# Attention and two MLPs on one Trainium2 core: another form of the first MLP's denominator, and a new written-out order

## The chip, the core and the metric

The kernel runs on one core of one Trainium2 chip. The metric is the device time of one launch in microseconds, as the median of the runs. A kernel's trace gives the time and place of every instruction of its engines: PE (TensorE matmuls), PEld (PE's weight loads), DVE (VectorE), ACT (ScalarE), POOL (GpSimd) and SP (SyncE, which issues the DMAs here).

## The reference

Three steps follow each other, on 1536 rows of 512 numbers (two batches of 768):

```python
# 1. attention, 8 heads of 64: 16 neighbours to each side, and one summary for each block of 32 keys
k_sum = k.reshape(B, H, nb, block, D).max(axis=3)
v_sum = v.reshape(B, H, nb, block, D).mean(axis=3)
...
x = softmax(concat(local scores, summary scores + log 32)) @ concat(v, v_sum)
# 2. the first MLP
h = x @ w_in                                   # 512 -> 2048
P = a[0] + a[1] * h + a[2] * h2 + a[3] * h3    # h2 = h*h, h3 = h2*h
Q = 1.0 + np.abs(b[0]) * np.abs(h) + np.abs(b[1]) * h2
x = (P / (Q + 1e-06)) @ w_out                  # 2048 -> 512
# 3. the second MLP, with the same weight shapes
h = x @ w_in
y = (h * np.clip(h + 3.0, 0.0, 6.0) / 6.0) @ w_out
```

## The kernel before

**Accuracy and pieces.** Every large matmul is done as three: a number is split into a high part (the program's type F32R) and a low rest, and high x low, low x high and high x high are summed in PSUM. One product of the first layer (`first_product`, L637) is 12 matmuls of 128x512 for 128 hidden features and 512 tokens; its four output pieces (`second_product`, L654) are 3 matmuls each. In the second MLP 7 products of a Strassen scheme replace 8 (`product`, L812), the third token chunk is done plainly (L939), and output pieces have line L850. Weights arrive as 64-bit numbers and are rebuilt by `convert` (a clamp on POOL or DVE, a Prelu on ACT, a shift L311 and an or L313 on DVE) and `split` (a cast L286 or L322 and a subtraction L325).

**Attention** works in 12 groups of 128 tokens, six of each batch. `scores(g)` (L507) puts 64 small matmuls into two PSUM banks; `top` (L520, DVE) adds the mask and takes the maximum; `softmax` does exp on ACT (L534), sums (also L538 on DVE), a guard 1e-9 (L546), a reciprocal (L552) and the division (L549); `turn` (L574) transposes the two halves on PE, with a copy out (L577, L578); `values` (L591) multiplies by v, and x is written as high and low part (L601, L603). Token chunk 0 is groups 0 to 3, chunk 1 groups 4 to 7 and chunk 2 groups 8 to 11. `bank()` gives the PSUM banks: the scores of groups 0 to 3 use the four y banks, the others hs2 and hs3, which values and the v averages use too.

**The averages of v** of the first batch (`v_sums0`, L432 and L434) are summed over all six v tiles in bank hs3, with a matrix of 1/32 that is loaded by DMA in two forms (`blkw_sb` and `blk_sb`; `consts2`). Four copies (L445) and one or two more (L452, L453) or small DMAs (L449) put them into the v tiles as rows 96 to 119. `v_sums1` (L471) does the second batch.

**The first MLP's activation** (`act1`) is run 16 times on one product of 128x512 (the first 16 products, n < SINGLE), then 16 times on a pair of 128x1024. It takes q = |h| from PSUM (L701, ACT), u = |b1| q + |b0| (L704 on POOL or DVE, L707 on ACT), q = q u (L717, POOL or DVE), t = a3 h + a2 (L721, ACT), two DVE steps with h from PSUM (L723, L724), 1/(1+q) by Ln and Exp on ACT (L728, L730) with a Newton step (L735, L737), the high part (L739, ACT) and the low part (`low`, L745).

**The order** is written out by hand. The program first lists all steps (`Plan.add`: an engine, planned microseconds, a function, what it reads and writes); some steps have several engines to choose from. `PICK` holds the choice for each of these, one digit each, and `ORDER` the order in which all steps are issued, two characters each. Every engine, SP's DMA queue among them, works through its own part of that order and waits where something that it needs is missing. The planned microseconds serve for that plan and for `idle`, which puts matmuls of zeros on PE (L1045, into a free bank) where the plan leaves PE idle for over 0.6 us.

**The tail.** `evac2` (L865) adds the last output pieces into `part` and stores each 128x512 piece (256 KB) on SP (L869).

Of the kernel before, what the change touches and what calls it, by code (L numbers as in the profile page):

```python
# [59 lines left out]
ORDER = (  # L60
    "###(#4#)#;#$#2#6#0#8#%%>#9#:#5#&%E#3#<#'#7#W#1%Z#V$&%?#?#B$(%@$7$'$.%A%F$8#=$)#@$9#A%L%H$Y%G$*$/%B$0"
    "$?%I#+$+$,&%$-$:$H$@$1$A&#$2%J$3$;&$$B%K$<$5$4$C&7$=%C$I#F#C$6$>%S$J$K#D&&#>$F#E$D&'$P%M#G$E%D$Z%N%#"
    "#H%$&0&)%O$L$Q&8$R%P#*#,$M&U&9#I&:%T'#%)$N%%&;#-%&%V$O&<#J$S%*%Q%'#K&=%+%U$T#.'H$G%($U#L#N$W$V#X#O%,"
    "#Z%W%.%-#P$#%2$X#Y#Q&3&Y&*#R%0&V&W%5&1%3&,#S%/%4%8%1'$%R%6%;%9%7%X#/'I':%<%:%Y(Y&+%=#T&2&-&>'J'K&4$%"
    "&.*X'L&5&/&?'M$$&@&D&(&Z&A&I'N&E&X+.+$&F(,&J&G&K&B'%&H*Y';&L&C')#M&M+%&N&6&P+/&O&Q+&*Z+2'<&R+0'.+#'*"
    "+<&S+3(-+''/(/+1(.&T#U+('B+4'&'++=+)'0+5',+*'-+J+@'1''+6'2'((H++'5+A+>'3+7'6+?+,'=+B(M(I+-,$+C'V'>+8"
    "'D+K(%+D+9'O'4+E+L'7+F+N+M(N+:+X+O'8(O,#+G(J+Q+;+Y'W,%'A+R+Z(P'Y,&'?'X,4'@'9'C+H(&,5(Z'Z,('P)#,2+I('"
    ")8'E(#(K+P(L(Q,3'G($'Q,E'F),(T(:,G(():(0(R(U+S,D(S'R,F)'+T(V'S+U(1,6()+V)()-,'(*).+W))(W'T(;)*)/,),X"
    "(2,:(X,Y(<(=)0)$,+,*)+(>'U,H)%,,)&,7(+(3)>,;,-,8(A)1)3(?,V)2)4(@,L,W,<)C)5)?,.,/,Z,9)6,I)@)D(6)E,0)7"
    ",J,=,M,K)A,>);,N)F,?,1,O-4)<)Q-#)O-&,@1Z)B)G)9)=(B-',P-1,A(C-2-(-5-$)J-8)P(D-3(4-%1L-0(5,Q)H,B-F-9)I"  # L70
    ',C)K-:-),R)Z(E(7-B-*,S)L-J-+-E,T*#-,-G-C,U)M(8-X-K)U-6)N--*$*%-7-D(9-Y)R.$)V-L)W1S-H-..%1M-;-U)X1O-I'
    "(F)S-W-<-T2%1N(G)T.6-M*&)Y2)-=*.-N*0-/*9-V->-O*'.1-?*(*).7-P...:-Q.0***:.&*/*;*4./-Z1P*+.8.;-R.H.#*<"
    ".<-@*,-A.'*-*5.22*1V*1.31T.(.4*6.L.Z*=*21U*3*G-S.).I*@*7.F/#.**8.5.X.+/&.E.9*L/'.D.M*>.J.W2#.=.V.K.>"
    '*H*M.N.G.,*?*A.Y*I.?2$/4*N.O.@.-.P.A*O.Q*B/5.R/$.S/3*E.B/%/(*F/1*C*J2&/8/2/6.T/F/9*K*P*D.C/)2,/*/7*S'
    "/0/+*T.U2+*Q/C1W*R/G/E/,/;*U/-/J/H/D/</I*V/W1Q*W/V1X/:1R/B/./K/X/M/=2I2'///N2-/>2./Y/L/O/?/P/@/U0&/Q"
    "0#2(0*052L2W0'/R0+0(0,/S0%060)2J/A0-2/0./T2X3&2K0/0$1Y0G0900080C2P/Z2Y010D0:070H020F0=0<0I0E0;030>0?"
    "2Z0J0R3)2M0K3#2N0L0@0S2O3$040A3'0M3%0U1$0N0T3X1(1%0X3J0Y0O1)1&143(1*3Y2Q0Q1'132R0B1+0P4#0V1,3*0Z1=1-"
# [1039 lines left out]
```

## Time and profile before

| | us |
|---|---|
| median of the 3 runs | 589.68 |
| the lowest and the highest | 589.3, 591.37 |
| the profiled execution | 589.21 |
| its span, from the first to the last instruction | 587.4 |
| PE busy / weight loads | 578.6 / 466.6 |
| DVE busy | 494.4 |
| ACT busy | 348.5 |
| POOL busy | 294.7 |

The profiled execution is 1.8 us longer than its span, and 0.5 us below the median. Matmuls are pipelined, so that PE's busy time says little about its pace; pace is read from how many matmuls end in a stretch. Idle time of an engine that does not hold the others up costs nothing.

### The profile page before, as it was taken

To read this page: it belongs to the slowest core of one execution; us is meant where nothing else is said; L and a number is where in the kernel's file an instruction comes from. 1 tells how busy PE (TensorE), PEld (TensorE's weight loads), DVE (VectorE), ACT (ScalarE), POOL (GpSimd) and SP (SyncE) were. 2 spreads that over 40 slices of the span, in tenths; PEclk is the share of its full clock that TensorE was granted. 3 is DMA by queue.
4 is the path that set the end of the run, shared out by engine and by line. 5 is a ranking of instruction groups with operands and counts; after the bars stand their busy time and mean duration, and the time that the engine had idled before them with its cause. 6 is when DMAs were issued, how large, how long until landed. Compare 5 with 4: busy or idle time off the path is not lost.

```text
span 587.4 us, 9645 instructions
## 1 busy us (share of the span) xinstructions
PE 578.6 (98%) x3608; PEld 466.6 (79%) x3613; DVE 494.4 (84%) x887; ACT 348.5 (59%) x648; POOL 294.7 (50%) x272
## 2 busy tenths in 40 slices
PE   8999999999999999999999999999999999999997
PEld 4477788888888888888888888888888888888886
DVE  5999999999989898988899998968687786866643
ACT  3988998988676677658657455524540434424410
POOL 1777676573475657654766472131423175523210
PEclk9999999999999999999999999999999999999999
DMA  8986534301222223110000141320313023002005
GB/s 311 352 306 209 192 118 151 104 30 35 73 71 73 76 101 110 37 36 2 17 20 1 37 143 37 107 73 0 144 32 113 1 73 126 18 0 73 1 1 214
DMA packets 17983, 53.10 MB, mean 90 GB/s; under 512 B 2273, under 2 KB 2785, under 8 KB 17937
## 3 DMA queue, kind: packets, MB, share of 16 engines
q1 hardware_dynamic: 17936, 52.49, 26.1%
q8 instruction: 28, 0.46, 0.3%
q14 instruction: 19, 0.15, 0.1%
HBM read 48.55 MB, written 3.15 MB: 88 GB/s over the span
## 4 chain that ended last, share of the span: by engine, by line
PE 94%; DMA 2%; DVE 1%; SPq 1%; issue 1%; POOL 0%; ACT 0%; DVEq 0%
PE y L654 23%; PE y L850 22%; PE hb L637 15%; PE hc L812 13%; PE hs L637 8%; PE hc L939 7%; PE hs L591 2%; PE hs L507 2%; PE hs L574 1%; DMA mask_sb<-in_masks 1%; DMA k<-in_blk 1%; SPq L280 1%; DVE s L520 0%; POOL s L549 0%; PE hs L434 0%
## 5 line engine op out<-in xcount | busy, mean ns | idle before, releaser
L654 PE MATMUL y<-g,wt 128*128 128x512 f32 x576 | 139.1, 392 | 0.0
L654 PEld LDWEIGHTS y<-g,wt 128*128 128x128 f32 x576 | 106.8, 188 | 22.3 <-POOL g L745 0.3
L850 PE MATMUL y<-wt,g 128*128 128x512 f32 x480 | 116.1, 389 | 0.0
L850 PEld LDWEIGHTS y<-wt,g 128*128 128x128 f32 x480 | 90.1, 188 | 18.7
L637 PE MATMUL hb<-xx,wt 128*128 128x512 f32 x384 | 89.5, 389 | 0.0
L325 POOL TENSOR_TENSOR wt<-raw,wt 128x512 fp32r<-128x512 f32 x44 | 62.4, 1425 | 51.0 <-DVE wt L322 30.4
L637 PEld LDWEIGHTS hb<-xx,wt 128*128 128x128 f32 x384 | 72.1, 188 | 15.0
L309 ACT ACTIVATE raw<-raw 128x512 f32<-128x512 f32 x62 | 41.1, 676 | 33.3 <-POOL raw L305 24.6
L717 POOL TENSOR_TENSOR q<-q,u 128x512 f32<-128x512 f32 x34 | 46.2, 1368 | 23.8 <-ACT u L707 14.4
L828 POOL TENSOR_TENSOR g<-t,g 128x512 fp32r<-128x512 f32 x17 | 23.4, 1380 | 63.3 <-ACT g L825 63.3
L825 ACT ACTIVATE g<-t 128x512 fp32r<-128x512 f32 x40 | 25.0, 628 | 49.4 <-PE y L850 43.4
L305 POOL TENSOR_SCALAR raw<-raw 128x512 f32<-128x512 f32 x44 | 35.8, 815 | 34.1 <-DMA raw<-in_w 33.9
L286 ACT ACTIVATE wt<-raw 128x512 fp32r<-128x512 f32 x56 | 36.8, 671 | 25.7 <-POOL raw L796 6.6
L313 DVE SCALAR_TENSOR_TENSOR raw<-raw 128x512 int32<-128x512 int32 x62 | 47.7, 779 | 4.3 <-ACT raw L309 4.1
L637 PE MATMUL hs<-xx,wt 128*128 128x512 f32 x192 | 47.8, 398 | 0.0
L812 PE MATMUL hc<-wt,wt 128*128 128x512 f32 x192 | 47.4, 389 | 0.0
L745 POOL TENSOR_TENSOR g<-t,g 128x512 fp32r<-128x512 f32 x22 | 30.6, 1397 | 30.3 <-ACT g L739 25.8
L939 PE MATMUL hc<-xx,wt 128*128 128x512 f32 x192 | 45.6, 389 | 0.0
L865 DVE SCALAR_TENSOR_TENSOR part<-y,part 128x512 f32<-128x512 f32 x36 | 24.4, 684 | 22.1 <-PE y L850 22.0
L939 PEld LDWEIGHTS hc<-xx,wt 128*128 128x128 f32 x192 | 36.0, 188 | 7.5
L812 PEld LDWEIGHTS hc<-wt,wt 128*128 128x128 f32 x192 | 36.0, 188 | 7.5
L637 PEld LDWEIGHTS hs<-xx,wt 128*128 128x128 f32 x192 | 35.1, 188 | 7.7 <-issue 0.2
(175 smaller groups left out, 1097.6 us busy)
## 6 DMA issues: line engine op xcount, KB each, us to landing
raw<-in_w SPq DMA_DIRECT2D x62, 512.0 KB, 4.2
vv<-in_vw SPq DMA_DIRECT2D x6, 512.0 KB, 7.1
out<-part SPq DMA_DIRECT2D x12, 256.0 KB, 2.9
k<-in_kT SPq DMA_DIRECT2D x4, 384.0 KB, 3.7
q<-in_qT SPq DMA_DIRECT2D x6, 256.0 KB, 7.5
e<-in_kT SPq DMA_DIRECT2D x4, 384.0 KB
raw<-in_vt SPq DMA_DIRECT2D x3, 512.0 KB, 5.1
e<-in_vw SPq DMA_DIRECT2D x3, 512.0 KB
```

What stands on the lines that cost most here:

```text
L286: nc.scalar.activation(out_, in_, AF.Copy)
L305: eng.tensor_scalar(out=hif, in0=hif, scalar1=CAP, scalar2=-CAP, op0=ALU.min, op1=ALU.max)
L309: add(ACT, 0.58, lambda: nc.scalar.activation(hif, hif, AF.Prelu, scale=REBIAS, alpha=2.0 ** 32), [kr], [(kr, 1)])
L313: add(DVE, 0.61, lambda: nc.vector.scalar_tensor_tensor(out=lo, in0=hi, scalar=3, in1=lo, op0=ALU.logical_shift_left, op1=ALU.bitwise_or), ...
L325: eng.tensor_tensor(out=to()[:, 1], in0=src, in1=to()[:, 0], op=ALU.subtract)
L637: mm(ps, lt, rt, start=(k == 0), stop=(k == 11))
L654: mm(y, lt, rt, start=(i == 0 and j == 0), stop=(i == HALF - 1 and j == 2))
L717: eng.tensor_tensor(out=q2[a][:, w], in0=q2[a][:, w], in1=u2[:, w], op=ALU.mult)
L745: eng.tensor_tensor(out=g2[a][:, 1, w], in0=t2[a][:, w], in1=g2[a][:, 0, w], op=ALU.subtract)
L812: mm(bank_at(bank_), left(lp, kk), right(rp, kk), start=(j == 0), stop=(j == 5))
L850: mm(yb[d], lt, rt, start=(j == 0 and e == 0), stop=(j == QUART - 1 and e == 2))
L939: mm(bank_at(2 * a + u), w_at(n)[:, lp, kk * P:(kk + 1) * P], x_of(2)[:, rp, kk, :], start=(j == 0), stop=(j == 11))
```

## The change

The denominator becomes q = |b0 h| (an Abs with a scale, ACT) plus u = (s h)^2 (a Square with a scale, ACT, from PSUM), with s the root of |b1|: the affine step is gone, the multiplication L717 becomes an addition on the same engines, and the first DVE step that reads h waits for both. The root is worked out once from b1, by Ln and Exp and a Newton step. The matrix of 1/32 for the last two v tiles is set by memsets on GpSimd, not loaded. The scores of groups 4 and 5 use the y banks. The very last output piece is added and stored in two halves. Planned durations are changed at many steps, and `PICK` and `ORDER` are new throughout.

```diff
-    '0000230000000000001100111010000000011100001100000000000001000000110000000101110000001010000000000010'
...
+    '0011330000120010001112111010111011100000100010100000010011000010000010000001110000100001110001201101'
...
-        dma(lambda: blk_sb, blk, 96, (), ["blk"])
+        add(POOL, 0.15, lambda: nc.gpsimd.memset(blk_sb, 0.0), (), ["blk"])
+        for c in range(P // BLK):
+            add(POOL, 0.1, lambda c=c: nc.gpsimd.memset(k_0[c * BLK:(c + 1) * BLK, 3616 + c:3808:32 + P // BLK], 1.0 / BLK), (), ["blk"])
...
-        dma(lambda: ab_in[:, 0:4], av.to_broadcast([P, 4]), 80, (), ["abi"])
-        dma(lambda: ab_in[:, 4:6], bv.to_broadcast([P, 2]), 80, (), ["abi2"])
+        dma(lambda: ab_in[:, 0:4], av.to_broadcast([P, 4]), 240, (), ["abi"])
+        dma(lambda: ab_in[:, 4:6], bv.to_broadcast([P, 2]), 240, (), ["abi2"])
...
+        add(DVE, 0.08, lambda: nc.vector.tensor_scalar_max(ab[:, 5:6], ab[:, 5:6], 1e-30), (), ["ab2"])
+        add(ACT, 0.12, lambda: nc.scalar.activation(rt[:, 0:1], ab[:, 5:6], AF.Ln), ["ab2"], ["rt"])
+        add(ACT, 0.12, lambda: nc.scalar.activation(rt[:, 0:1], rt[:, 0:1], AF.Exp, scale=0.5), (), ["rt"])
+        add(DVE, 0.08, lambda: nc.vector.reciprocal(out=rt[:, 1:2], in_=rt[:, 0:1]), (), ["rt"])
+        add(DVE, 0.08, lambda: nc.vector.scalar_tensor_tensor(
+            out=rt[:, 0:1], in0=rt[:, 1:2], scalar=ab[:, 5:6], in1=rt[:, 0:1], op0=ALU.mult, op1=ALU.add), ["ab2"], ["rt"])
+        add(DVE, 0.08, lambda: nc.vector.tensor_scalar_mul(ab[:, 6:7], rt[:, 0:1], 0.5), ["rt"], ["ab3"])
...
-        if g < 4 and kind == "s":
-            n = 2 * (g % 2) + j
+        if g < 6 and kind == "s":
+            n = 2 * (g % 2 if g < 4 else 5 - g) + j
...
-        add(ACT, us_of(0.5, 0.93), lambda: nc.scalar.activation(q, psum(), AF.Abs), hk, qk + ak)
...
-        lins = [(POOL, us_of(0.73, 1.17), lambda: lin(nc.gpsimd), True), (ACT, us_of(0.71, 1.15), lin_a, False),
-                (DVE, us_of(0.46, 0.73), lambda: lin(nc.vector), True)]
...
+        add(ACT, us_of(0.573, 1.0), lambda: nc.scalar.activation(q, psum(), AF.Abs, scale=ab[:, 4:5]), hk + ["ab2"], qk + ak)
+
+        add(ACT, us_of(0.573, 1.0), lambda: nc.scalar.activation(uu, psum(), AF.Square, scale=ab[:, 6:7]), hk + ["ab3"], uk + bk)
...
-                eng.tensor_tensor(out=q2[a][:, w], in0=q2[a][:, w], in1=u2[:, w], op=ALU.mult)
+                eng.tensor_tensor(out=q2[a][:, w], in0=q2[a][:, w], in1=u2[:, w], op=ALU.add)
...
-        add(DVE, us_of(0.6, 1.14), lambda: nc.vector.tensor_tensor(out=t, in0=t, in1=psum(), op=ALU.mult), hk + ak, tk)
+        add(DVE, us_of(0.71, 1.255), lambda: nc.vector.tensor_tensor(out=t, in0=t, in1=psum(), op=ALU.mult), hk + ak + bk, tk)
...
-        add(DVE, 0.61, lambda: nc.vector.scalar_tensor_tensor(
-            out=pt, in0=y, scalar=1.0 / 6.0, in1=pt, op0=ALU.mult, op1=ALU.add), yk, pk)
-        if r == 3:
-            r0 = c * N + d * P
-            add(SP, 0.45, lambda: nc.sync.dma_start(out[r0:r0 + P, :], pt), pk, (), land=0.66)
+        cuts = (slice(0, N),) if (r, c, d) != (3, 2, 3) else (slice(0, N // 2), slice(N // 2, N))
+        for v in cuts:
+            part_key = pk if len(cuts) == 1 else [("p", c, d, v.start)]
+            add(DVE, 0.61 / len(cuts) + 0.03 * (len(cuts) - 1), lambda v=v: nc.vector.scalar_tensor_tensor(
+                out=pt[:, v], in0=y[:, v], scalar=1.0 / 6.0, in1=pt[:, v], op0=ALU.mult, op1=ALU.add), yk + pk * (len(cuts) - 1), part_key)
+            if r == 3:
+                r0 = c * N + d * P
+                add(SP, 0.45, lambda v=v: nc.sync.dma_start(out[r0:r0 + P, v], pt[:, v]), part_key, (), land=0.66 / len(cuts))
```

Decoded from `PICK`, the engines' shares over the whole kernel change so: the guard of the softmax from 20 on POOL and 4 on DVE to 6 and 18; the casts of `split` from 62 on ACT and 26 on DVE to 54 and 34, its subtractions from 48 on POOL and 40 on DVE to 40 and 48; the step L717 from 34 on POOL and 14 on DVE to 36 and 12. Decoded from `ORDER`, PE's first steps in either order are these (z zeros, S scores, t a transpose, m and M averages of the first and second batch, V values, F a first product, y an output piece):

```
before  zzzzSSSSttmttmmmmmtttVtVVVS FS FttV FS FttM FV yyyyyyyS yyt yt yyV FyyS Ftt
after   zzzzSSStSttmtmSmtmmmttVtVVVSt Ft FV FS Ftt yMV yyyFS yyytt FV yyyyyS yyyyFtt
```

## Rows read from the trace of the kernel before

**Rows 1.** Busy us by stage: PE, PEld, DVE, ACT, POOL; clock, DMA share, GB/s.
```profile
0.00:10.00 10.00, 8.53 (x79) 3.81 (x82) 4.05 (x5) 1.28 (x1) 0.69 (x7) 1.00 0.80 269
10.00:20.00 10.00, 8.40 (x229) 6.06 (x225) 9.26 (x55) 9.17 (x31) 6.29 (x10) 1.00 1.04 395
20.00:30.00 10.00, 9.68 (x31) 2.96 (x29) 9.57 (x39) 9.68 (x36) 7.49 (x14) 1.00 0.98 333
30.00:40.00 10.00, 8.68 (x212) 6.88 (x211) 9.87 (x18) 8.73 (x17) 7.46 (x8) 1.00 0.98 319
40.00:150.00 110.00, 109.49 (x1165) 88.20 (x1163) 105.17 (x284) 101.27 (x264) 73.76 (x72) 1.00 0.37 122
150.00:330.00 180.00, 180.00 (x795) 148.81 (x794) 164.69 (x187) 119.90 (x140) 110.40 (x89) 1.00 0.16 53
330.00:584.00 254.00, 253.81 (x1120) 209.83 (x1118) 191.21 (x304) 98.45 (x164) 88.63 (x75) 1.00 0.19 65
```

**Rows 2.** Chain of waits, the head: start us, us, what held it.
```profile
3.54 6.93 DMA mask_sb<-in_masks
...
21.45 6.15 DMA k<-in_blk
27.73 1.88 PE hs L434 x4
...
34.44 1.87 PE hs L591 x64
...
38.79 1.25 PE hs L507 x64
40.04 2.94 PE hs L637 x12
...
84.97 0.87 PE hs L574 x8
```

**Rows 3.** Timelines of ACT and of DVE before F0: start us, us, instruction.
```profile
29.64 2.03 ACT L445 COPY vv<-hs 24x512 f32<-24x512 f32 x4 [0.32 <-PE hs L434]
...
36.71 1.27 DVE L603 TENSOR_TENSOR xx<-hs,xx 128x512 fp32r<-128x512 f32 x2
```

**Rows 4.** Groups of DVE by form, 0 to 40 us: busy us, mean ns.
```profile
L520 DVE CUSTOM_DVE_ANT_0 s<-y,mask_sb 128x120 f32<-128x120 f32 x24 | 5.1, 276 | 1.5 <-DMA mask_sb<-in_masks 1.5
...
L376 DVE TENSOR_REDUCE ks<-k 128x24 f32<-128x768 f32 x4 | 3.8, 953 | 4.2 <-DMA k<-in_kT 4.2
...
L578 DVE COPY t<-hs 120x512 f32<-120x512 f32 x2 | 1.4, 688 | 0.1
...
L538 DVE TENSOR_REDUCE stat<-e 128x4 f32<-128x480 f32 x2 | 1.3, 634 | 0.0
...
L322 DVE CAST wt<-t 128x512 fp32r<-128x512 f32 x1 | 0.4, 426 | 0.0
```

**Rows 5.** The chain of waits, later: start us, us, what held it.
```profile
103.63 1.58 PE y L654 x6
...
112.14 2.72 PE hs L637 x12
...
149.85 5.44 PE hb L637 x24
...
562.73 21.09 PE y L850 x93
583.85 0.69 DVE part L865
```

**Rows 6.** Groups by form, whole kernel: busy us, mean ns of one.
```profile
L704 POOL TENSOR_SCALAR u<-q,ab 128x512 f32<-128x512 f32 x13 | 12.5, 965 | 9.6 <-DVE t L737 8.5 <-PE hs L574 0.7 <-ACT q L701 0.3
L721 ACT ACTIVATE t<-hs,ab 128x512 f32<-128x512 f32 x16 | 12.4, 775 | 0.4 <-PE hs L637 0.4
L701 ACT ACTIVATE q<-hs 128x512 f32<-128x512 f32 x16 | 9.4, 590 | 2.9 <-PE hs L637 2.8
```

**Rows 7.** L311 on DVE: mean (by form), and min, median and max ns.
```profile
L311 DVE TENSOR_SCALAR raw<-raw 128x512 int32<-128x512 int32 x62 | 33.5, 547 | 4.2 <-DMA raw<-in_w 4.1
...
L311 DVE TENSOR_SCALAR raw<-raw x62: 412/421/1518, 12.2 to 545.7; 128x512 int32<-128x512 int32 x62
```

**Rows 8.** DMA issues: out<-in, count, KB each, median us to landing.
```profile
out<-part SPq DMA_DIRECT2D x12, 256.0 KB, 2.9
```

More of the change, by code (lines that the diff above doesn't have):

```diff
@@ L74 @@
[L74 to L77, printed above, removed]
-    "0W1A1#1>1.153K181?161/1<1:1B10193Z1@11203L1C121D3M2S171E4$222T211F2U4%3+1G3,1H1;2:4&4'263N2>3-2V4U1I"
@@ L444, in v_sums0 @@
                 for w in range(2):
-                    add(ACT, 0.48, lambda to=to, w=w: nc.scalar.copy(to[:, w], ps[96:96 + NB, :]),
+                    add(ACT, 0.6, lambda to=to, w=w: nc.scalar.copy(to[:, w], ps[96:96 + NB, :]),
                         (), [("h", 3), (("v", g), w)],
@@ L508, in go @@
                                q[hd, p, w * 64:(w + 1) * 64], rhs, start=True, stop=True)
-        add(PE, 1.3, go, [qk] + [("k", b, p) for p in range(4)] + [("ks", b, p) for p in range(4)],
+        add(PE, 1.25, go, [qk] + [("k", b, p) for p in range(4)] + [("ks", b, p) for p in range(4)],
             [sc[0][1], sc[1][1]], fresh=(sc[0][1], sc[1][1]))
@@ L549, in share @@
                 eng.tensor_tensor(out=s, in0=s, in1=sm[:, 2, j].to_broadcast([P, NPAIR, KW]), op=ALU.mult)
-            add(POOL, 0.2, lambda f=guard: f(nc.gpsimd), (), [km], port=True, more=[(DVE, 0.08, lambda f=guard: f(nc.vector), True)])
+            add(POOL, 0.6, lambda f=guard: f(nc.gpsimd), (), [km], port=True, more=[(DVE, 0.08, lambda f=guard: f(nc.vector), True)])
             add(DVE, 0.09, lambda j=j: nc.vector.reciprocal(out=sm[:, 2, j], in_=sm[:, 1, j]), (), [km])
@@ L574, in go @@
                     nc.tensor.transpose(ps[:KW, p * P:(p + 1) * P], s[:, p, :], id_sb)
-            add(PE, 0.43, go, [("s", n), "id"], [key], fresh=(key,))
+            add(PE, 0.355, go, [("s", n), "id"], [key], fresh=(key,))
             add(ACT, 0.48, lambda pt=pt, ps=ps: nc.scalar.copy(pt[:KW, :], ps[:KW, :]), [key], [pk],
@@ L593, in go @@
                            start=True, stop=True)
-        add(PE, 1.07, go, [vk, (vk, 0), (vk, 1), pt[0][1], pt[1][1]], [key], fresh=(key,))
+        add(PE, 1.08, go, [vk, (vk, 0), (vk, 1), pt[0][1], pt[1][1]], [key], fresh=(key,))
         pv = ps.rearrange("p (a n) -> p a n", n=P)
@@ L734, in act1 @@
             out=t, in0=t, scalar=ab[:, 0:1], in1=r(), op0=ALU.add, op1=ALU.mult), rk, tk, port=not two)
-        add(DVE, us_of(0.61, 1.14), lambda: nc.vector.scalar_tensor_tensor(
+        add(DVE, us_of(0.61, 1.25), lambda: nc.vector.scalar_tensor_tensor(
             out=r(), in0=q, scalar=C1, in1=r(), op0=ALU.add, op1=ALU.mult), qk, rk, port=not two)
@@ L738, in act1 @@
             out=t, in0=r(), scalar=2.0, in1=t, op0=ALU.subtract, op1=ALU.mult), rk, tk, port=not two)
-        add(ACT, us_of(0.53, 0.95), lambda: nc.scalar.activation(gh, t, AF.Copy), tk, gk)
+        add(ACT, us_of(0.53, 0.97), lambda: nc.scalar.activation(gh, t, AF.Copy), tk, gk)
         low(a, us)
```

118 lines of the change are left out of this document (58 added, 60 removed).

## The prediction

> **What bounds the kernel now.** I read the stage table first [rows 1]. The granted clock is 1.00 in every stage, TensorE's upper level of 2.4 GHz, so the clock explains nothing. From 150 to 584 us TensorE (PE) issues without a break: 795 matmuls in 180.0 us and 1120 in 254.0, 0.227 us each. The two ends of that stretch in the chain of waits say the same: 24 matmuls in 5.44 us at 149.85 and 93 in 21.09 at 562.73 [rows 5]. The change takes no matmul away, so those 434 us can be made longer but not shorter. What can be won lies ahead of 150 us and behind the last matmul.
>
> Then the chain of waits of the head [rows 2]. It is held by transfers: the mask lands at 3.54 + 6.93 = 10.47, and the averaging matrix blk at 21.45 + 6.15 = 27.60, where the last of the v averages begins on PE. The DMA engines are full all that time (share 1.04, 0.98, 0.98 from 10 to 40 us at 395, 333 and 319 GB/s [rows 1]). Behind it come four ACT copies (29.64 to 31.67 [rows 3]), the four value products (the last ends at 34.44 + 1.87 = 36.31), and the last x piece on DVE (36.71 + 1.27 = 37.98 [rows 3]). Filler matmuls and issue time go up to 38.79, a score group takes 1.25, and the first MoE product, F0, starts at 40.04.
>
> From F0 to the first paired product at 149.85 are 109.8 us. PE's list there, decoded from the order string, is 16 F at 2.72, 50 output pieces at 0.68, 7 score groups at 1.25, 16 transposes at 0.44 (0.87 for two), 8 value products at 0.94 (1.87 for two) and the one average of the second batch, put at 1.25 by estimate: 43.5 + 34.0 + 8.8 + 7.0 + 7.5 + 1.3 = 102.1 [rows 2, 5]. A run of MoE matmuls that follows an attention piece pays once more: 12 take 2.94 instead of 2.72, and 6 take 1.58 instead of 6 x 0.227 = 1.36, so 0.22 a time [rows 2, 5]. The order has 28 such changes of kind: 6.2 us. 109.8 - 102.1 - 6.2 leaves 1.5 us of real stalls. DVE is busy 105.2 of 110 us there and ACT 101.3 [rows 1]: nearly full, but they hold PE up little.
>
> **The changes of kind.** In the changed order I count 23 of them, since score groups, transposes and value products stand next to each other more often. 5 x 0.22 = 1.1 us less, all on the path. The one way in which this is worth nothing is that PE waits at the same places for data anyway.
>
> **The head, up to F0.** The averaging matrix needs no transfer now. The clearing memset and the four small ones on GpSimd are free: POOL is busy 0.69 us of the first 10 [rows 1]; were they late, the last two averages would wait for them, tenths of a microsecond. But blk is not the last block any more. In the new DMA order the second v block of the averages is the last that they need. Up to it the queue holds two more weight blocks (512 KiB each), one more query block and that v block (256 each), less blk (96): some 9900 KiB (the tiny a and b loads left out) against 8460 up to blk before. 1440 KiB more at 333 GB/s [rows 1] are 4.3 us, so it lands at about 32 instead of 27.6. The averages end about 33.2 (one half of 1.88 behind it [rows 2]). The copies are now split between ACT and DVE, half of 2.03 [rows 3]: values start at 34.3, and take what they took, 29.6 + 2.1 = 31.7 to 36.3, so they end at 38.9. Scores of group 5 and one transpose (1.25 + 0.44) now stand between the values and F0, in the hole of 1.7 us that x leaves (36.31 to 37.98): the other banks make that possible, because they need not wait for a bank that the last values still occupy. By transfers F0 starts at about 41.
>
> By DVE it is later. Everything that DVE's list puts ahead of F0 grows by: two score reductions (24 instructions of [rows 4] in 5.1 us are six, 0.85 each), two exp sums (0.63), two v copies (0.69 each, by the nearest copy) and three casts (0.43), a shift and ten tiny ones (about 1.5); less one key maximum (0.95), one copy and one multiplication (0.7 each). 1.7 + 1.3 + 1.4 + 1.3 + 1.5 - 2.4 = 4.8, and I take 4.5. DVE has little idle time before 38 us (9.57 and 9.87 busy of the last two tens [rows 1]), so x and group 4's softmax are ready at 38.0 + 4.5 = 42.5, and a little sooner if the idle 0.5 us is used: F0 at 42.2. It has 1.7 us more of PE's work ahead of it than before, so that 41.7 would be even. I take a loss of 0.5, from a gain of 1 (the transfers' 41) to a loss of 2 (DVE a tenth slower on this list and no idle time used).
>
> **The denominator.** Per 512 columns it removes one affine step (13 on POOL at 0.965 us in this stretch [rows 6], the rest on DVE and ACT) and adds one Square on ACT from PSUM. The trace has no Square and no Abs with a scale from memory; the bounds are the plain Abs from the same bank (0.59) and the Identity with scale and bias from memory (0.775) [rows 6]. I take 0.65, nearer to the first, since only one operand is added. 16 x 0.65 = 10.4 us more on ACT before 150 us, and 16 x 0.06 = 1 for the scale. The choices of engine take back two affine steps on ACT and five casts (7 x 0.7 = 4.9), and the v copies that leave ACT another 1.5; tiny steps add 0.5. So ACT's load grows by about 5.5 us over the first 150 (130.2 now, 28.9 + 101.3 [rows 1]), of which 3.7 ahead of F0 and 1.8 behind it. DVE's grows by about 3, POOL's falls by about 6. Beside PE that fits, but closely: ACT has 8.7 us idle between 40 and 150, and 103.1 in some 108 us is a share of 0.95. Behind 150 us it fits easily: ACT is busy 119.9 of 180 us and the Square of a pair replaces an affine step that ran in the same place. DVE's first multiplication now waits for Square as well; queued behind it are DVE's other steps of that product, and the score reductions of the next group. If ACT comes to each product at once that costs nothing.
>
> Of the 1.5 us of stalls behind F0 I take 0.4 away, because scores 4 and 5 and a transpose are done ahead; bounds are all 1.5 gone, or 3 more.
>
> **The small constants.** Six tiny ACT and DVE steps work out the scale of Square, the root of |b1|, before the first product: tenths of a microsecond, hidden before 40 us unless the b load is late, and it is moved up to the ninth place of SP's queue.
>
> **The tail.** The last matmul is followed by 0.69 us of DVE (583.85 [rows 5]), and a store of 256 KB that takes 2.9 us to land [rows 8]. In halves the last one carries 128 KB. DVE ends no sooner (two pieces of 0.36 to 0.4), SP issues the second directly behind the first. What is saved is the transfer of half a block, 128 KB at 333 to 395 GB/s [rows 1], 0.3 to 0.4 us; I take 0.3, with 0 as the other bound.
>
> **Sum.** -1.1 (changes of kind) + 0.5 (F0) - 0.4 (stalls) - 0.3 (tail) = -1.3 us. The profiled execution took 589.2 with a span of 587.4; the median of the runs is 589.7. I make it 588.4 against that median.
>
> **Rivals.** *DVE gets shorter.* A shift on DVE, L311, takes 421 ns in the median but 547 in the mean and up to 1518 [rows 7]: the long ones are waits within the instruction, and 62 of them lose 62 x 0.126 = 7.8 us. If POOL's instructions cause these, fewer of them shorten DVE's list, in which the shift is one of many kinds. POOL's work falls by 6 us of 95.7 (21.9 + 73.8 [rows 1]) ahead of 150. With F0 at 41 (-0.7 against the even point) and no stalls behind it the sum is -1.1 - 0.7 - 1.5 - 0.3 = -3.6, and up to 1 us more if DVE saves a tenth of what it waits: 585 to 586.1. The Trainium skill, SBUF — State Buffer, section "SBUF: two separate sides", says that DVE and GpSimd share a port pair under an exclusive lock, and that the loser waits for the whole instruction. By that rule it is this sum, without it the forecast's; the spread of L311 agrees with the rule, but no row shows how many of these waits the removed instructions cause.
>
> *ACT becomes the bound, and it is slower.* The point from which this decides is ACT's share between F0 and the first pair: 101.3 of 110 now, 0.92; the forecast needs 0.95. If waiting in order keeps it at 0.92, 103.1 us of work take 112, +2, and with F0 and the tail it is 592; at 0.90 they take 114.6, +4.6, and it is 594.5. For it speaks that Square lies between the bank and DVE's first multiplication and holds the bank 0.65 us longer; against it that ACT was at 0.97 for a stretch (9.68 of 10 [rows 1]) and that there is one F in each 6 to 7 us and two banks for it. The Trainium skill, PSUM — Partial Sum Buffer, section "PSUM bank collisions raise a hardware error", says that two engines must never access one bank at the same time, reads included. By this rule DVE's multiplication can't run beside Square, and the 0.65 us is paid on that chain; no row of before shows it.
>
> *It does not do what it says.* The blk transfer that is saved buys nothing, since a later block lands at 32: that is in the forecast already. If SP is also held by the two reloads of weight buffers that stand ahead of v blocks (each waits for its conversion), the transfers have a hole of 2 to 4 us and F0 comes at 44 to 46: 590 to 592.5.
>
> **How the numbers follow.** The forecast, between 587 and 590: 0.46. DVE shorter, below 587: 0.27. Transfers with a hole, 590 to 592.5: 0.12. ACT as the bound, 591.5 and more: 0.15, of which 0.14 above 592.6. This kernel's measurement can tell about 0.5%, 2.9 us, from no change: faster is below 586.8, slower above 592.6. Faster 0.26, same 0.60, slower 0.14. The range 585.3 to 592.8 leaves out a little of the first rival and most of what lies beyond ACT's 0.92.
>
> **What would show it.** In the trace after: PE without a gap from about 148 us on; 23 runs of MoE matmuls that begin 0.22 late; F0 at 41 to 43 with a score group right ahead of it; no blk transfer and the v block landing near 32; Square at 0.6 to 0.75; the last store some 0.3 us sooner. I am wrong if F0 starts before 40, if PE has gaps behind 150, or if ACT is the releaser of PE's waits.

## The result, and the profile after

| | before | after |
|---|---|---|
| median of 6 runs each, us | 589.92 | 595.91 |
| the profiled execution, us | 589.21 | 596.07 |
| its span, us | 587.4 | 594.3 |

The ratio is 1.0088, with a 95% interval of 1.0059 to 1.0118: 0.9% slower. The prediction said 588.4, within 585.3 and 592.8. It was wrong.

The stage table after (busy us of PE, PEld, DVE, ACT, POOL; granted clock, DMA share, GB/s), to be laid beside [rows 1]:

```profile
10.00:20.00 10.00, 8.96 (x210) 5.63 (x202) 9.10 (x48) 7.89 (x32) 4.27 (x7) 1.00 1.03 377
20.00:30.00 10.00, 9.74 (x155) 5.31 (x157) 10.00 (x50) 9.81 (x32) 6.72 (x11) 1.00 0.95 332
30.00:40.00 10.00, 9.16 (x93) 4.72 (x94) 9.86 (x36) 8.90 (x29) 8.15 (x10) 1.00 0.84 288
40.00:150.00 110.00, 106.44 (x1177) 86.79 (x1175) 103.66 (x275) 100.12 (x239) 61.83 (x58) 0.98 0.39 125
150.00:330.00 180.00, 180.00 (x824) 148.88 (x824) 159.33 (x189) 132.32 (x153) 90.31 (x78) 1.00 0.16 51
```

From 40 to 150 us PE is busy 106.4 us where it was 109.5, and the granted clock is 0.98 there and no longer 1.00. The chain of waits of the head (start us, us, what held it), beside [rows 2]:

```profile
3.52 7.73 DMA mask_sb<-in_masks
...
24.08 2.73 POOL wt L326 x2
...
27.21 0.43 SPq L281
...
42.67 1.15 PE y L518 x50
43.82 2.07 issue
45.90 0.47 PE y L518 x9
46.37 0.58 PE hs L585 x4
46.95 4.35 PE hs L648 x12
```

F0, the first MoE product, starts at 46.95 (40.04 before) and takes 4.35 us (2.94 before). Ahead of it PE stops for 2.07 us in the middle of group 5's scores, and the chain has no releaser for that, only "issue": time in which the engine waited for nothing that the profile shows. SP stood until POOL's 2.73 us were over before it could issue the second v block at 27.21.

How late PE is at each point against its own list (the times of [rows 2, 5], as the prediction used them) shows where the 6.9 us of span come from: 5.2 us at the start of F0, 0.9 in F0 and the piece behind it, -0.6 from there to the first paired product, 1.4 behind that. Together 6.9. By the clock alone the stretch from the first paired product to the last matmul takes as long as before (434.2 and 434.1 us in the records). But the new order has 52 output pieces ahead of that product and not 50, so 1.4 us less is left for PE behind it, and these 1.4 us are lost there.

### The profile page after: what moved, and what is told of

Read it like the earlier page. It is cut to its first block, busy times and chain, and to the rows that moved or that the text cites. A ratio compares the mean times of both kernels' runs of the same rounds, so it can differ in the third digit from the quotient of the medians.

```text
span 594.3 us, 9650 instructions
## 1 busy us (share of the span) xinstructions
PE 582.9 (98%) x3619; PEld 468.3 (79%) x3624; DVE 496.5 (84%) x917; ACT 360.0 (61%) x645; POOL 261.3 (44%) x245
## 4 chain that ended last, share of the span: by engine, by line
PE 84%; DVE 7%; DMA 2%; issue 2%; ACT 2%; POOL 1%; SPq 1%; DVEq 0%; ACTq 0%; POOLq 0%
PE y L850 21%; PE y L665 21%; PE hb L648 15%; PE hc L812 12%; PE hs L648 6%; PE hc L942 5%; DMA mask_sb<-in_masks 1%; PE hs L602 1%; DMA ab_in<-in_av 1%; DVE s L531 1%; PE hs L585 1%; PE hs L518 1%; SPq L281 1%; POOL raw L796 1%; DVE u L735 1%
## 5 line engine op out<-in xcount | busy, mean ns | idle before, releaser
L326 POOL TENSOR_TENSOR wt<-raw,wt 128x512 fp32r<-128x512 f32 x37 | 52.6, 1432 | 58.9 <-ACT wt L287 31.3
L717 POOL TENSOR_TENSOR q<-q,u 128x512 f32<-128x512 f32 x36 | 47.3, 1325 | 43.9 <-ACT q L712 23.5
L287 ACT ACTIVATE wt<-raw 128x512 fp32r<-128x512 f32 x49 | 32.0, 673 | 30.4 <-DVE raw L314 11.1
L745 POOL TENSOR_TENSOR g<-t,g 128x512 fp32r<-128x512 f32 x22 | 29.9, 1363 | 38.6 <-ACT g L739 34.7
L648 PEld LDWEIGHTS hs<-xx,wt 128*128 128x128 f32 x192 | 36.4, 194 | 9.0 <-DVE t L724 1.3
L868 DVE SCALAR_TENSOR_TENSOR part<-y,part 128x512 f32<-128x512 f32 (+1 forms) x37 | 24.3, 670 | 22.1 <-PE y L850 22.1
```

The lines of the kernel that those rows point to most:

```text
L287: nc.scalar.activation(out_, in_, AF.Copy)
L326: eng.tensor_tensor(out=to()[:, 1], in0=src, in1=to()[:, 0], op=ALU.subtract)
L648: mm(ps, lt, rt, start=(k == 0), stop=(k == 11))
L717: eng.tensor_tensor(out=q2[a][:, w], in0=q2[a][:, w], in1=u2[:, w], op=ALU.add)
L745: eng.tensor_tensor(out=g2[a][:, 1, w], in0=t2[a][:, w], in1=g2[a][:, 0, w], op=ALU.subtract)
```

## The experiments

Times are medians beside the kernel before on the same chip, which took 589.96 to 590.34 in these runs. Line numbers shift by up to 26 in the kernels with added code; the tiles' names don't. "p" is the start of the first paired product, 149.7 us before and 156.6 after.

### Shifted instructions, and the parts alone

Two runs moved PE's instruction count by 128, in the changed kernel and in the kernel before; 8 large matmuls of zeros in the start-up become 72 small ones, and nothing else changes:

```diff
-            add(PE, 1.5, lambda: [mm(hs[2], z[:, :P], z, start=True, stop=True) for _ in range(4)],
+            add(PE, 1.5, lambda n=n: [mm(hs[2][:, 0:w], z[:, :P], z[:, 0:w], start=True, stop=True)
+                                      for w in ([N] * 4 if n < 2 else [16] * 36)],
```

> The changed kernel with 128 more PE instructions ahead of everything (64 more small matmuls of zeros, 8 large ones less, while PE waits for its first data). Nothing else moves. Theory A, starved instructions: PE's own instructions come by DMA in blocks of 256; the 2.07 us in which PE stood still within the scores of group 5 (43.8 to 45.9 us) was such a block that came late behind the data transfers, and the half clock of the 3.4 us behind it followed from that pause. Shifted by half a block, the border falls between other instructions: no pause there, first product F0 at about 44.5 in place of 46.95 and done in 2.95 instead of 4.35 us, time 592 (2.4 + 1.4 less than 595.9). Rival B, late elementwise work: x and the banks were late anyway, the pause hides behind that, and what is gained at F0 is lost again at the waits for banks behind it: 595 to 596. Rival C, the denominator: as B, 595 to 596.

> The kernel before with the same 128 PE instructions more ahead of everything. A: its own late block (0.9 us at 37.5) fell into the time in which x was missing anyway, so 589.5 to 590.5, and the trace shows the pauses at other instructions. B and C: no change, 589.9. Over 592 would say that the border of a block decides in this kernel too.

Measured: 595.28 (ratio 1.0084, 1.0063 to 1.0105) for the changed kernel, 597.41 (1.0121, 1.0098 to 1.0144) for the kernel before. Both miss. In the changed kernel the pause within group 5's scores is gone and F0 takes 3.0 us at full clock, but two other pauses, 1.2 us at 15.2 and 1.6 us at 23.6, have come, and it gains 0.6 us where 4 were expected. The kernel before, with every other engine's work as it was, loses 7 us by 128 small instructions in its start-up. Its waits of PE from 10 to 60 us (us in total, times, longest), and the stages around them:

```profile
PE y L508 <- issue: 3.4, 1, 3.4
PE hs L508 <- issue: 1.8, 1, 1.8
PE hs L1046 <- issue: 1.0, 1, 1.0
```

```profile
15.00:20.00 5.00, 2.83 (x127) 2.47 (x127) 3.74 (x11) 2.94 (x9) 4.10 (x5) 1.00 1.01 372
20.00:30.00 10.00, 8.81 (x31) 3.44 (x31) 6.72 (x37) 6.83 (x28) 4.03 (x10) 0.83 0.94 312
40.00:50.00 10.00, 7.97 (x115) 5.99 (x112) 8.95 (x29) 8.16 (x23) 7.74 (x9) 0.83 0.62 231
```

In the records the three pauses stand behind the 449th, the 705th and the 1217th of PE (matmuls, weight loads and waits of its sequencer): 256 and 2 x 256 apart. In the changed kernel the one at 43.82 stands behind the 1213th; five matmul records are missing from that trace, and in e9, e11 and e12, where none is, the same pause stands behind the 1217th. The page lists where the instructions come from: a DMA queue of its own, 28 packets for 7,243 matmuls and weight loads.

```profile
q8 instruction: 28, 0.46, 0.3%
```

One packet in 259 instructions, 16 KB each (29 packets in e1 and e2, which have 128 more): PE's program arrives in blocks of 256 instructions, by DMA like the data. That was not in the prediction at all.

The other two runs put parts of the change into the kernel before, in its own order: Abs and Square alone (with Square in the place of the affine step, and 24 steps moved to where their inputs exist), and everything but the denominator and the order (the matrix by memsets, the other banks, the last store in halves).

```diff
-        (eng, took, fn, port), more = lins[0], lins[1:]
-        add(eng, took, fn, qk + ["ab2"], uk, port=port, more=more)
+        square = lambda: nc.scalar.activation(uu, psum(), AF.Square, scale=ab[:, 6:7])
+        add(ACT, took, square, hk + ["ab3"], uk + bk, more=[(ACT, took, square, False)] * 2)
```

> The kernel before in its own order with the denominator of the change alone: Abs with a scale, Square on ACT in the place of the affine step (24 of 2181 steps move up so that no step precedes what it needs), addition in the place of the multiplication. C, the denominator costs by itself (Square on ACT, the bank held longer): 592.5 to 595 with PE waiting for banks or for ACT's results between 60 and 330 us. A and B: 589.5 to 591, since ACT has 8.7 us idle between 40 and 150.

> The kernel before in its own order with the other three edits: the averaging matrix by memsets, the scores of groups 4 and 5 in the y banks, the last store in halves. A and B: 0.3 us at the end and up to 1 at the head (the block of 96 KB less in the queue, score group 4 not waiting for a bank): 588.6 to 589.8. If one of them does harm, over 591.

Measured: 617.19 (1.0458, 1.0433 to 1.0483) with Square; 590.09 (0.9996, 0.9983 to 1.0009) with the three small edits, which are therefore neither the loss nor a gain. No theory had expected as much as 27 us from Square; they are followed up below (e16).

### Who is late: transfers, DVE's list, or the pause

A function (`shifted`) takes steps out of the written-out order and puts them back right ahead of another step; PE's fillers stay as they were. Four runs use it on the changed kernel: the scores of group 5 behind F0, the v loads ahead of the two weight reloads for which SP stands, these and the mask sooner, and all three. The call of e8 has all three moves; e5 has the last of them, e6 the first, e7 the first two:

```diff
+        seq = plan.shifted(seq, [([57, 35, 36, 37, 38], 198), ([22], 149), ([455, 208, 223, 209], 224)])
```

> The changed kernel with one move on PE: the scores of group 5 and the transpose behind them stand behind the first MoE product F0 instead of ahead of it; the score reduction on DVE moves with them by one place. Fillers stay. In the trace of the changed kernel PE pauses 2.07 us within these scores (43.82 to 45.90, at instruction 1213 of its list, while the packet with the next 256 instructions lands at 44.17), x is ready at 44.03, F0 starts at 46.95 and takes 4.35 at half clock instead of 2.94. Theory A (PE starved of instructions, then half clock): F0 starts at 44.1 to 44.4 and the border falls inside or behind it; what is saved is up to 2.07 + 1.41 = 3.5 us, less 0.2 to 0.4 for changes of kind: 592.5 to 593.5 beside 595.9 for the changed kernel. Rival: the pause goes along with the border, stops F0 itself for as long, and the clock falls all the same: 595 to 596.

> The changed kernel with one move on SP's queue: the five v loads that stand between and behind the two reloads of weight buffers are issued ahead of the first of these, for which SP stood from 17.3 to 21.0 (the second from 24.1 to 26.8). Theory T (transfers with a hole, the third rival of the prediction): the second v block lands near 29 instead of 33.7, the averages end near 31 instead of 35.64, F0 comes 2 to 4 us sooner: 592 to 594 beside 595.9. Theory L (DVE's list holds F0, the second term of the prediction's head): DVE is busy from the mask's landing at 11.25 to x at 44.03 with under 1 us idle, so x comes at most 0.7 sooner and the time is 595 to 596. Theory A adds: with fewer loads left for 40 to 45 us the instruction packet may be there in time; then 3 us less whatever else.

> The same five v loads moved, and the mask's load issued one place sooner, ahead of the first weight load of 512 KB. Theory L: DVE's list starts at the mask (first score reduction at 11.39), so the mask lands near 10 and x is ready 1.0 to 1.5 us sooner than in the run with the v loads alone: 1 to 1.5 us less than that. Theory T: no difference from that run, since the v block lands at the same time; within 0.4 us of it.

> All three moves in the changed kernel: v loads, mask, and the scores of group 5 with their transpose behind F0. If A and L both hold, x at 42.3 to 43, F0 there, no pause ahead of it and full clock: 5 us less than the changed kernel, 590.5 to 591.5. If only A holds: 592.5 to 593.5. If neither: 595 to 596.

Measured: 596.55 (1.0106), 596.09 (1.0103), 597.34 (1.0115), 598.17 (1.0136). Nothing is won by any of them, and e7 and e8 are worse than any theory had it. Theory A missed in e5 though its first half came true: F0's first matmul started at 43.4 (46.7 in the changed kernel), and F0 took 3.0 us from its first start to its last end and not 4.6. But DVE's next work is the reduction of group 5's scores, and it stood still for them (DVE's waits from 10 to 60 us):

```profile
DVE s L553 <- PE y L540: 4.4, 1, 4.4
```

So it is not F0 that the rest hangs on here, but DVE. Theory T fell in e6: with the v loads early, values began no sooner (37.8 against 36.8), since what they wait for comes from DVE, and DVE now waited for the weight load that had been moved back (PE's and DVE's waits, 10 to 60 us):

```profile
PE hs L607 <- DVE stat L579: 1.7, 1, 1.7
```

```profile
DVE raw L334 <- DMA raw<-in_w: 2.1, 2, 1.3
```

With the mask sooner as well (e7) values began at 40.4. In its profiled execution, the longest of the six, the granted clock was at half from 32.2 us on for 6.8 us, behind a wait of PE of 1.6 us for DVE, and the last four averages took 3.6 us and not 1.9. The pause stayed in e6 (1.4 us) and e7 (2.5).

### DVE's load up to the first paired product

Busy us of PE, PEld, DVE, ACT and POOL from 0 to p: before, then after.

```profile
0.00:149.69 149.69, 144.47 (x1695) 107.64 (x1700) 137.62 (x397) 129.82 (x346) 95.39 (x109) 1.00 0.52 177
```

```profile
0.00:156.57 156.57, 149.00 (x1711) 110.94 (x1717) 141.55 (x419) 134.09 (x340) 84.75 (x96) 0.99 0.50 169
```

DVE's busy and idle time add up to p: 137.6 + 12.1 before, 141.6 + 15.0 after. About half of that idle time lies ahead of the mask; behind it DVE is idle 5.5 us before and 7.9 after. So the 6.9 us are 3.9 of work, 2.4 of idle time behind the mask and some 0.6 ahead of it (the mask landed at 11.25 in this execution). The idle time behind the mask grows by as much as the wait for group 5's scores, while PE pauses (DVE's waits in the changed kernel, 40 to 160 us):

```profile
DVE s L531 <- PE y L518: 2.4, 1, 2.4
```

Such a sum proves nothing by itself: busy and idle time add up to p for every engine, and ACT's busy time rose by 4.3 us as well. Nor is all of the 3.9 new work; ahead of p the new order has 16 products through L724 and L733, where the old one had 15. Four runs change DVE's or ACT's load without touching order or PE's list: 18 guards on DVE left out; guards and sums in the kernel before on the engines that the changed kernel uses; guards, sums and v copies in the changed kernel on the engines of before; Square cut to one column.

```diff
-            add(POOL, 0.6, lambda f=guard: f(nc.gpsimd), (), [km], port=True, more=[(DVE, 0.08, lambda f=guard: f(nc.vector), True)])
+            add(POOL, 0.6, lambda f=guard: f(nc.gpsimd), (), [km], port=True, more=[(DVE, 0.08, lambda: None, True)])
```

This is e9; in e10 and e11 only digits of `PICK` differ; and e12 has

```diff
-        add(ACT, us_of(0.573, 1.0), lambda: nc.scalar.activation(uu, psum(), AF.Square, scale=ab[:, 6:7]), hk + ["ab3"], uk + bk)
+        add(ACT, us_of(0.573, 1.0), lambda: nc.scalar.activation(uu[:, 0:1, 0:1] if two else uu[:, 0:1], psum()[:, 0:1, 0:1] if two else psum()[:, 0:1], AF.Square, scale=ab[:, 6:7]), hk + ["ab3"], uk + bk)
...
-                eng.tensor_tensor(out=q2[a][:, w], in0=q2[a][:, w], in1=u2[:, w], op=ALU.add)
+                eng.tensor_tensor(out=q2[a][:, w], in0=q2[a][:, w], in1=q2[a][:, w], op=ALU.add)
```

> The changed kernel without those 18 of its 24 guards (adding 1e-9 to the softmax sums) that stand on DVE; nothing takes their place, PE's list is the same. They take 3.4 us of DVE up to the first paired product. Theory L (DVE's list is the bound from the mask to the first paired product: it is idle for 7.9 of 146 us there in the changed kernel, and its work up to there is 141.8 us against 137.8 before): the first paired product starts 2.5 to 3.4 us sooner (at 153.2 to 154 instead of 156.6), time 592.5 to 593.5. Theory A (pauses for PE's instructions hold the head): they stay, 595 to 596.

> The kernel before with the changed kernel's choice of engine for two kinds of softmax step, the guards (14 more on DVE, net, at 0.19 us) and the sums (4 more on DVE, net, at 0.56, with ACT's exp shorter by the accumulations); order and everything else as before. DVE gets 4.9 us more up to the first paired product, POOL and ACT less. Theory L: of the 5.5 us that DVE is idle there some 1.5 take up part of it, and the rest shows: 593 to 595 beside 590. Rival R (DVE nearly full but not the bound, as the prediction had it): 589.5 to 591.

> The changed kernel with the kernel before's choice of engine for guards, sums and v copies: DVE loses 6.2 us up to the first paired product, ACT gains some 2.8, POOL some 7. Order as in the changed kernel. Theory L: 591 to 592.5, less than the full 6 since ACT, idle for 7 us between F0 and the first pair, comes next. If ACT is the bound (second rival of the prediction): 594.5 to 597, no gain or a loss. Theory A: 595 to 596.

> The changed kernel with the Square cut to one column (its work is left out, its place, its waits and its issue stay; the addition reads |b0 h| twice instead). ACT loses 0.6 us for each of the 16 single products, 9.6 up to the first pair. Second rival of the prediction (ACT, with Square, is the bound, or Square holds the bank): 591 to 593. Theory L: ACT's load isn't the bound, 595 to 596.

Measured: 594.70 (1.0071, 1.0053 to 1.0088), 596.07 (1.0100, 1.0080 to 1.0119), 597.11 (1.0114, 1.0094 to 1.0133), 596.49 (1.0106). The same view for e10, and for e11 and e12:

```profile
0.00:155.57 155.57, 145.93 (x1699) 107.32 (x1700) 145.57 (x415) 129.12 (x330) 89.83 (x95) 1.00 0.50 171
```

```profile
0.00:157.47 157.47, 149.14 (x1716) 110.85 (x1717) 135.44 (x399) 137.70 (x359) 89.24 (x109) 0.99 0.50 168
```

```profile
0.00:154.30 154.30, 147.97 (x1717) 109.81 (x1717) 141.16 (x419) 127.90 (x340) 84.14 (x96) 1.00 0.52 172
```

e10 shows that DVE holds p in the order of before: 8.0 us more of DVE's time (4.9 were expected; the guards alone took 479 ns in the mean and not 190), less on ACT and POOL, p 5.9 us later, time 6.1 longer. e12 speaks against ACT as what holds the changed kernel: 6.2 us less on ACT brought nothing in the median (p came 2.3 us sooner in its profiled execution, in which the clock did not fall). e9 went half the way of theory L: 3.0 us less work, but 1.6 more idle time, with the pause still there (2.2 us). e11 missed: 6.1 us less on DVE, but ACT, which took them, was late with the v copies (PE waited 1.9 us for one), and the pause was 2.5. An order made for one choice of engines can lose by another choice, even one that is lighter for DVE.

### The pause taken away

Packets of PE's instructions between 28 and 50 us, start to landing, from the records of queue 8:

```
after       30.73 to 31.64    43.24 to 44.17    48.63 to 49.72
e13         30.09 to 30.96    40.21 to 41.24    46.87 to 47.80
```

PE goes on at 45.90, 1.7 us behind the landing at 44.17. It had entered the block ahead of the pause at 39.58 and was through with its 256 instructions 4.0 us later; the next block's packet began 3.7 us behind that entry. At 99.88 us, with a DMA share of 0.19 in the ten us that follow, PE enters a block as well, and a packet begins 0.6 us behind. To let the packet come sooner, e13 moves five loads that nobody needs before 55 us behind one that waits; e14 also leaves out all guards; e15 leaves them out of the kernel before.

```diff
+        seq = plan.shifted(seq, [([236, 267, 46, 258, 367], 259)])
-            add(POOL, 0.6, lambda f=guard: f(nc.gpsimd), (), [km], port=True, more=[(DVE, 0.08, lambda f=guard: f(nc.vector), True)])
+            add(POOL, 0.6, lambda: None, (), [km], port=True, more=[(DVE, 0.08, lambda: None, True)])
```

> The changed kernel with five of SP's loads (1.9 MB, none needed before 55 us) moved behind a load that waits for the value products' time, so that they no longer fill the DMA engines when the packet with PE's instructions from 1213 on is due (it is called for near 39 us and starts only at 43.24). PE's list and all other engines' lists are as in the changed kernel. Theory A: the packet comes in time, group 5's scores run without the 2.07 us pause, DVE's 2.37 us of idle time at 44.03 and the half clock are gone: first paired product 2 to 2.6 us sooner, time 593 to 594. Rival: the pause isn't due to the transfers and stays, or a later load is now missed: 595.5 or more.

> The same, and all 24 guards are left out (sums of exponentials of which one is 1 do not change by 1e-9 in this number format). If pause and DVE's work add up (A and L): 2 to 2.6 from the one and 2.5 to 3.4 from the other, 590 to 591.5. If DVE's lighter list only exposes another wait: no better than 593.

> The kernel before without its 24 guards (20 on POOL, 4 on DVE). DVE loses 1.1 us up to the first paired product; each softmax loses a hop to POOL and back. L: 588.5 to 589.5. If the hops hold DVE up: 587 to 588.5. If the order absorbs both: 590.

Measured: 592.55 (1.0046, 1.0029 to 1.0062), 591.38 (1.0023, 1.0011 to 1.0036), 589.68 (0.9991, 0.9976 to 1.0005). Theory A holds in e13, and a little better than expected: five loads moved, 3.4 us less. e15 cannot be told from the kernel before. The stage in which the packet is due, after and in e13:

```profile
39.00:42.00 3.00, 2.45 (x76) 2.34 (x78) 2.94 (x6) 2.55 (x6) 2.82 (x4) 1.00 0.93 344
```

```profile
39.00:41.30 2.30, 1.87 (x64) 1.76 (x62) 2.23 (x6) 1.74 (x4) 1.98 (x3) 1.00 0.20 69
```

With the DMA engines at 0.20 and not at 0.93 the packet landed 2.9 us sooner, the scores ran through, F0 started at 43.6 and took 3.0 us at full clock. And the two causes add up: p came at 155.1 in e9, without the guards on DVE, at 152.50 in e13, with the loads moved, and at 150.73 in e14, with both.

```profile
0.00:150.73 150.73, 147.22 (x1717) 109.66 (x1717) 139.96 (x401) 133.67 (x340) 83.82 (x90) 1.00 0.53 176
```

The Trainium skill, Runtime: NRT & Kernel Launch, section "Instruction fetch mechanics", says that an engine's instructions are refilled in 16 KiB blocks of 256 by a DMA queue of its own, and that crossing a block's border is mostly hidden. The packets and their spacing agree. That it is hidden does not hold here, where small matmuls use up 256 instructions in 4.0 us beside full DMA engines.

### Why Square alone cost 27 us

Square cut to one column, in the order of before:

> The run with Abs and Square alone in the order of before, with Square cut to one column (its work is left out, its place and waits stay; the addition reads |b0 h| twice). That run took 617.2. If ACT's load made it so long, ACT loses 0.69 us for each single product and 1.1 for each pair, and it falls to 592 to 598. If it is the waiting in order (ACT stands at Square until DVE's last Newton step of an earlier product has read the buffer that it writes, 9.9 us of idle time, and all that is queued behind it on ACT stands too): 605 or more.

Measured: 605.99 (1.0282, 1.0258 to 1.0305), at the lower end of what waiting in order was to give. 11 us of the 27 go with Square's work and 16 stay without it. The single Square in e3, in e16 and in the changed kernel (busy us, mean ns | idle time ahead of it and its releaser):

```profile
L738 ACT ACTIVATE u<-hs,ab 128x512 f32<-128x512 f32 x16 | 10.9, 686 | 9.9 <-DVE t L763 9.9
```

```profile
L738 ACT ACTIVATE u<-hs,ab 128x1 f32<-128x1 f32 x16 | 4.0, 259 | 10.3 <-DVE t L763 10.3
```

```profile
L714 ACT ACTIVATE u<-hs,ab 128x512 f32<-128x512 f32 x16 | 10.9, 683 | 1.3 <-DVE t L737 1.3
```

It writes a buffer that DVE's last Newton step of an earlier product still reads. On POOL that wait cost little (the affine step had it too: 8.5 us [rows 6]); on ACT exp, copies and the next product's Abs stand behind it. The new order leaves 1.3 us of it. So this denominator needs another order. That the new order pays for it with DVE's longer list is a reading; no run separates the two.

### Work handed from DVE to POOL

e14 still has 2.3 us more of DVE's work up to p than before. Two runs give some to POOL, idle for 44% of that time: the seven low parts (`low`, L745 in the changed kernel), then also four subtractions (L326).

> The changed kernel with the five loads later and without guards (591.4), and with the seven low parts (L745) that DVE works out up to the first paired product given to POOL: DVE loses 7 x 0.79 = 5.5 us there, POOL gains 7 x 1.37. If DVE's list is still the bound and POOL (idle for half of that time) comes to them in time: the first paired product 2.5 to 4 us sooner (DVE's idle time takes the rest), 588 to 589. If PE's output pieces wait for POOL's longer low part, or ACT is the next bound at once: 590.5 to 592.

> The same, and the four subtractions of weights (L326) that DVE does up to there also given to POOL (2.7 us more off DVE, two of them ahead of F0). If the head is held by DVE: another 0.5 to 1.5 us, 587 to 588.5. If POOL's order or the weights become late: 590.5 or more.

Measured: 593.08 (1.0045, 1.0029 to 1.0061) and 595.98 (1.0089, 1.0067 to 1.0112); both worse than e14. DVE lost 5.5 us of steps in e17 and its busy time fell by 0.6 only (139.96 to 139.34); in e18 it lost 8.2 and the time rose to 141.62. Three DVE steps by form, up to p, in e14, e17 and e18 (busy us, mean ns). In these kernels L336 is the "or" of `convert`, L759 the last Newton step, and L745 the first step that reads h from PSUM:

```profile
L336 DVE SCALAR_TENSOR_TENSOR raw<-raw 128x512 int32<-128x512 int32 x18 | 13.8, 772 | 0.1
L759 DVE SCALAR_TENSOR_TENSOR t<-u,t 128x512 f32<-128x512 f32 x14 | 11.0, 790 | 0.0
L745 DVE TENSOR_TENSOR t<-t,hs 128x512 f32<-128x512 f32 x16 | 10.8, 676 | 0.6 <-ACT q L734 0.5
```

```profile
L336 DVE SCALAR_TENSOR_TENSOR raw<-raw 128x512 int32<-128x512 int32 x18 | 15.8, 883 | 0.4 <-ACT raw L332 0.3
L759 DVE SCALAR_TENSOR_TENSOR t<-u,t 128x512 f32<-128x512 f32 x14 | 12.2, 874 | 0.0
L745 DVE TENSOR_TENSOR t<-t,hs 128x512 f32<-128x512 f32 x16 | 10.8, 677 | 1.2 <-ACT q L734 1.2
```

```profile
L336 DVE SCALAR_TENSOR_TENSOR raw<-raw 128x512 int32<-128x512 int32 x18 | 15.7, 874 | 1.4 <-ACT raw L332 1.3
L759 DVE SCALAR_TENSOR_TENSOR t<-u,t 128x512 f32<-128x512 f32 x14 | 13.0, 932 | 0.0
L745 DVE TENSOR_TENSOR t<-t,hs 128x512 f32<-128x512 f32 x16 | 10.8, 676 | 1.0 <-ACT q L734 1.0
```

The two that work from SBUF to SBUF got longer, by 84 to 142 ns each; the one that reads a PSUM bank did not. POOL's 9.6 us more went with about 5 us more on DVE's other steps in e17. The Trainium skill, SBUF — State Buffer, section "SBUF: two separate sides", says that DVE and GpSimd share a port pair and the loser waits out the whole instruction, for DVE steps with two SBUF inputs among others. The rows agree in which steps got longer; that a whole instruction is waited out they do not show. And p came 1.6 us later in e17 though DVE's busy time fell: DVE was idle 2.2 us longer, and its waits for ACT's results in the activation rose from 1.2 to 2.9 us.

## Why the prediction was wrong

In short: the forecast set the head at +0.5 us and everything else at a gain. The head lost 5.2, by DVE's longer list and by a pause of PE for its own instructions, which it did not have. One run took away the pause (e13), one a part of the list (e9), and e14, with both, is 1.4 us behind the kernel before where the changed kernel is 6.0.

**"+ 0.5 (F0)"** is the step that failed most: measured +5.2 at F0 (start at 46.95, beside the even point of 41.7), and +1.4 for F0 itself. Two things are in it. By the records F0's first matmul starts at 46.70 in the changed kernel, at 43.61 without the pause (e13) and at 41.97 without the pause and without any guard (e14).
- The rival's clause on a hole in SP's queue came true in its facts (SP stood until 26.83, the averages ended at 35.64 and not at 33.2), but e6 shows that this was not what held x. DVE's list was: predicted to give x at 42.5, it gave it at 44.03. The list was forecast 4.5 us longer ahead of F0; DVE's busy time from 0 to F0 rose by 4.1, and the mask came 0.8 later in this execution. This part was right, with the upper end of the bound.
- The pause for instructions was missing. It was in the kernel before too, and visible: "issue" of 0.91 us up to 38.40, ahead of F0, behind the 957th record, 256 ahead of the 1213th. For half of it x, which came at 37.98, was missing anyway. I read it as a part of the hole. In the changed list it falls into group 5's scores, and DVE waits for those: 2.4 us, and the clock's fall on top.

**"nearly full, but they hold PE up little"** is the reading of [rows 1] that failed, for DVE. DVE's 105.2 of 110 us was taken as cover, because PE shows 1.5 us of stalls. But PE's list is made of what DVE lets through, in an order searched for that. e10 shows the price: 5.9 of 8.0 us that DVE got more. "DVE's grows by about 3" was nearly the right size (3.9); "Beside PE that fits" was the wrong price: nothing, where e10 paid three quarters. The other way the price does not hold: e9 took 3.0 us off DVE and gained 1.2, e11 took 6.1 and gained nothing.

**Changes of kind and stalls, -1.1 and -0.4:** the counts of 28 and 23 are right. But from the second MoE product to the first pair PE lost 6.2 us against its list, 6.8 before: -0.6. One new stall ate most of the rest; PE waits for a bank (its waits, 40 to 160 us):

```profile
PE y L518 <- issue: 2.1, 1, 2.1
PE hs L648 <- DVE t L724: 1.0, 1, 1.0
```

**The tail, -0.3:** the last matmul ends 3.5 us before the end in both (590.78 to 594.3; 583.85 to 587.4). Gain 0.0, the other bound; in e4 the time didn't move either.

**"those 434 us can be made longer but not shorter":** the prediction took PE's list there as unchanged. It is two output pieces, 1.4 us, shorter, and the stretch takes as long as before. The 1.4 us go in waits of 0.1 to 0.4 us each, near 331, 374 to 377 and 495 us. No run tells which of the later choices makes them.

**The rivals.** *ACT as the bound* had the right sign, but not the cause (e12). Square took 0.683 for the 0.65 assumed. None of the three signs of being wrong came: F0 was not early, ACT was not what PE waited for, and behind 150 the profile shows a single wait of PE, of 0.2 us. *DVE gets shorter*: its mechanism is there. With 10.6 us less on POOL up to p the shift L311 (L312 after) on its 18 raw tiles, 643 ns in the mean before, took 487 (before, then after):

```profile
L311 DVE TENSOR_SCALAR raw<-raw 128x512 int32<-128x512 int32 x18 | 11.6, 643 | 0.0
L312 DVE TENSOR_SCALAR raw<-raw 128x512 int32<-128x512 int32 x18 | 8.8, 487 | 0.6 <-DMA raw<-in_w 0.6
```

That is 2.8 us, but more than that was added, by the time up to DVE's next step: 14 guards (2.4 us), 4 sums (2.3), two v copies (1.4), five casts (1.6).

**What stays open:** e14 is 1.4 us behind the kernel before (1.0 at p, the rest behind it), and the waits behind 330 us are not assigned. No version tried beats the kernel before: the best, e15, is at 0.9991 with 1 inside its interval.

## What to carry to other kernels

An engine that is busy for 95% of a stage can bound it even if the profile shows PE hardly waiting, as DVE did here. Price what a change adds to its list at nearly full, and do not count on getting the same back for what it takes away. Moving a step to an idle engine is no gain by itself: in e17 POOL's added 9.6 us went with most of DVE's 5.5 coming back, and an order made for one choice of engines lost 1 us under one that was lighter for DVE. Where small matmuls run beside full DMA engines, look in the trace for "issue" on PE and for the packets of its instructions, and keep loads that can wait out of that moment.
